# Attention and a residual MLP on one core: final evictions on VectorE in place, the pair's RELU in three parts, a PSUM tile for each Y product, u of batch 0 kept on the chip

## The chip, the core and the metric

The kernel runs on one NeuronCore of a Trainium2 chip. The core has a matrix engine (TensorE, PE in the profile, with its weight loads as PEld), a vector engine (VectorE, DVE), a scalar engine (ScalarE, ACT), GpSimd (POOL) and SyncE (SP), which here only starts transfers. Each engine works through its own list of instructions in order and waits at semaphores for the others. Transfers are started from SP's list (most of them) and from POOL's (those that also turn f32 into bf16). The metric is the device time of one execution, in microseconds (us).

## The reference

For each of 8 batches, 16 query heads and 4 key and value heads of 64 columns attend over 384 tokens; the result x is 384 x 1024. An MLP with two residuals follows.

```python
a1 = alpha1 * x + beta1
tok = np.einsum('ts,bsd->btd', w_tok, a1)
u = x + lam * tok
a2 = alpha2 * u + beta2
ch = np.maximum(a2 @ w_ch1, 0.0) @ w_ch2
return (u + lam * ch).astype(np.float32)
```

w_ch1 is 1024 x 4096, w_ch2 is 4096 x 1024. All inputs and the output are f32 in HBM.

## The kernel before

The two products with w_ch1 and w_ch2 are most of the work. The attention of a batch up to u (function `side`) is cut into small pieces that are put between the matmuls of an earlier batch's MLP. The places are written out by hand in a table `plan`: its key is a stage, a phase (0 for w_ch1, 1 for w_ch2) and a slot, and each `yield` of `main` or `pair` is one slot. The order of every engine's list is the order in which the Python code runs.

The program in time: a lead (attention of batch 0), `main(0)` and `main(1)` (MLP of batches 0 and 1), then `pair(0)`, `pair(1)`, `pair(2)` (MLP of batches 2 and 3, 4 and 5, 6 and 7). A `pair` takes two batches through a product as a 2 x 2 block matrix, by seven block products instead of eight; the numbers 1 to 7 in `SEQ1` and `PLACE2` are these products. The sums of blocks that they need are made by DVE: `sums_a` for the activations, `sum_w1` for w_ch1, `sum_w2` for w_ch2. The sums of w_ch2 are written to HBM once (`w2s`), and each pair fetches them (`fetch`).

Phase 0 of a pair has 8 groups g of 14 slots. A slot is one product o for one of two columns e of blocks: four matmuls into PSUM. Products 1, 6, 5 and 3 go on adding into one tile X[e]; after 1, 6 and 5 ACT copies what is there so far (`snap`, line L612), and the next product may only then write on. Products 7 and 4 add into Y, and product 2 uses Z. DVE adds snaps to Y and Z and writes the results into `hid` (L614, L616, L620). At the end of a group one ACT instruction applies RELU to three blocks of both columns (L627), and DVE forms two more blocks (L628, L629). The ring of six slots `w1` holds chunks of w_ch1 (POOL loads, L170) or blocks of w2s (SP fetches, L577); `free` takes the next load from `queue` as soon as a slot's last matmul is written down.

Phase 1 has the seven products in order 1, 5, 6, 3, 7, 4, 2, each as two halves h of three row tiles ms: 84 slots of four matmuls. Products 3, 7, 4 and 2 end an output block. For each ms DVE takes the product out of PSUM (L668, or L670 with a snap added). What is left of the final step runs on POOL: times lam (L671, not for product 3) and plus u (L672). Then SP stores the tile (L474). The three u tiles are loaded by SP at the start of the half h = 1 (L470). For the last output block of the last pair, DVE does L671 and L672 too.

In phase 1 `side` of two batches runs between the products. For each of its eight parts p: scores (PE, L265), exp (ACT, L274), `av` (PE, L304, then four DVE instructions, L309 to L319), `tok_flip` (PE, L329, then DVE L336 and L340). SP then stores u (`spill`, L229) and starts a transpose by DMA into `ops` (L353). The tile behind L340 has two buffers, so L340 of part p waits until the transpose of part p - 2 has landed. `sums_a` (L531 to L534) reads the transposed blocks. `load_next` loads q, k and v of a batch on POOL's list, and `put_flips` places their transposes on SP's list (L157, L161).

## Time and profile before

| What | Before |
|---|---|
| Median of 3 runs (lowest, highest) | 913.31 us (910.75, 914.59) |
| The profiled execution | 914.28 us, its span 912.5 us |
| Mean granted TensorE clock of that execution | 0.954 |
| Busy: ACT, POOL | 348.5 us, 231.7 us |
| Moved by DMA | 165.66 MB, mean 182 GB/s |

The span runs from the first to the last instruction. Busy time of PE comes from matmuls that overlap, so a full PE stands for matmuls back to back and not for the engine's peak. A wait is shown as the idle time of an engine ahead of an instruction, with the instruction that ended it behind an arrow. A granted clock under 1.00 means that TensorE was given fewer clock pulses in that stretch.

### The profile page before, as it was taken

To read this page: it belongs to the slowest core of one execution; us is meant where nothing else is said; L and a number is where in the kernel's file an instruction comes from. 1 tells how busy PE (TensorE), PEld (TensorE's weight loads), DVE (VectorE), ACT (ScalarE), POOL (GpSimd) and SP (SyncE) were. 2 spreads that over 40 slices of the span, in tenths; PEclk is the share of its full clock that TensorE was granted. 3 is DMA by queue.
4 is the path that set the end of the run, shared out by engine and by line. 5 is a ranking of instruction groups with operands and counts; after the bars stand their busy time and mean duration, and the time that the engine had idled before them with its cause. 6 is when DMAs were issued, how large, how long until landed. Compare 5 with 4: busy or idle time off the path is not lost. (4 is left out here: it accounts for less than half of the span.)

```text
span 912.5 us, 14496 instructions
## 1 busy us (share of the span) xinstructions
PE 765.9 (84%) x5707; PEld 418.8 (46%) x5707; DVE 495.9 (54%) x918; ACT 348.5 (38%) x465; POOL 231.7 (25%) x247
## 2 busy tenths in 40 slices
PE   8899998988958777999667678899894777779994
PEld 5655554654534444454333344445452344444441
DVE  7553562554786655486435655537664665554113
ACT  7422324643304555543210355564331145552100
POOL 8333204202003110003553531000434431100352
PEclk9999999999988999999977799999998889999998
DMA  9999999999978972468989998426887977725675
GB/s 191 207 210 203 221 197 217 208 213 214 291 212 165 212 93 92 143 199 220 234 226 168 166 145 114 113 94 191 205 270 222 179 117 93 93 93 172 214 252 191
DMA packets 231136, 165.66 MB, mean 182 GB/s; under 512 B 93588, under 2 KB 203780, under 8 KB 231068
## 3 DMA queue, kind: packets, MB, share of 16 engines
q0 software_dynamic: 114688, 54.37, 46.6%
q1 hardware_dynamic: 115836, 109.98, 42.2%
q8 instruction: 44, 0.72, 0.3%
q10 hardware_dynamic: 544, 0.39, 0.1%
q14 instruction: 24, 0.20, 0.1%
HBM read 166.63 MB, written 39.85 MB: 226 GB/s over the span
## 5 line engine op out<-in xcount | busy, mean ns | idle before, releaser
L647 PE MATMUL C<-w,arena 128*128 128x512 bf16 x1008 | 239.9, 385 | 1.5 <-DMA w<-w2s 1.5
L274 ACT ACTIVATE es<-sc 128x1024 bf16<-128x1024 f32 x126 | 121.8, 1022 | 201.7 <-PE sc L265 192.6
L647 PEld LDWEIGHTS <-arena 128*128 128x128 bf16 x1008 | 93.1, 99 | 107.6 <-issue 13.1
L612 ACT ACTIVATE hT<-X,bias 128x384 f32<-128x384 f32 x144 | 80.9, 577 | 102.4 <-PE X L607 83.6
L170 POOL DMA_DIRECT2D w<-in_moe_w_ch_dram x68 | 60.4, 892 | 218.2 <-PE X L607 161.2
L607 PEld LDWEIGHTS <-w 128*128 128x128 bf16 x768 | 76.3, 100 | 73.5 <-issue 21.6
L607 PEld LDWEIGHTS <-ws 128*128 128x128 bf16 x576 | 57.3, 99 | 105.4 <-issue 72.6
L607 PE MATMUL X<-ops,ws 128*128 128x384 bf16 x384 | 73.9, 337 | 27.8 <-ACT hT L612 27.8
L487 PE MATMUL h<-ops,w 128*128 128x384 bf16 (+1 forms) x480 | 87.5, 336 | 10.9 <-DMA ops<-a 3.9
L517 PE MATMUL ch<-arena,hT 128*128 128x512 bf16 x384 | 91.5, 383 | 1.5 <-DMA arena<-in_moe_w_ch_dram 1.5
L607 PE MATMUL X<-ops,w 128*128 128x384 bf16 x384 | 73.1, 334 | 14.7 <-DVE o L523 9.1
L627 ACT ACTIVATE arena<-arena 128x2304 bf16<-128x2304 bf16 x24 | 50.9, 2123 | 76.4 <-DVE arena L620 76.4
L660 POOL TENSOR_TENSOR hT<-hT 128x512 f32<-128x512 f32 x9 | 13.4, 1493 | 215.4 <-ACT hT L658 215.4
L487 PEld LDWEIGHTS <-w 128*128 128x128 bf16 x480 | 46.2, 100 | 43.8 <-issue 9.6
L672 POOL TENSOR_TENSOR o<-o,ut 128x512 f32<-128x512 f32 x33 | 45.0, 1371 | 79.6 <-DMA ut<-us 63.8
L607 PE MATMUL Y<-ops,ws 128*128 128x384 bf16 x192 | 39.0, 325 | 24.3 <-DVE arena L620 24.3
L304 PEld LDWEIGHTS <-es 128*128 128x128 bf16 x1008 | 39.6, 99 | 42.1 <-issue 31.0
L517 PEld LDWEIGHTS <-hT 128*128 128x128 bf16 x384 | 35.2, 98 | 39.9 <-issue 5.2
L614 DVE TENSOR_TENSOR arena<-Y,hT 128x384 bf16<-128x384 f32 x48 | 26.8, 558 | 44.0 <-ACT hT L612 41.8
L265 PE MATMUL sc<-qT,kT 64*128 64x384 bf16 (+2 forms) x576 | 45.5, 276 | 5.7 <-DVE xr L312 2.9
L340 DVE TENSOR_TENSOR a<-xr,vecs 128x384 bf16<-128x384 f32 x56 | 38.3, 685 | 20.1 <-DMA ops<-a 18.2
L607 PE MATMUL Y<-ops,w 128*128 128x384 bf16 x192 | 42.1, 342 | 8.5 <-DVE ops L534 5.3
(128 smaller groups left out, 908.9 us busy)
## 6 DMA issues: line engine op xcount, KB each, us to landing
w<-w2s SPq DMA_DIRECT2D x84, 512.0 KB, 4.1
w<-in_moe_w_ch_dram POOLq DMA_DIRECT2D x68, 512.0 KB, 8.9
ut<-us SPq DMA_DIRECT2D x48, 256.0 KB, 6.2
out_dram<-o SPq DMA_DIRECT2D x48, 256.0 KB, 2.1
us<-xr SPq DMA_DIRECT2D x56, 192.0 KB, 4.0
arena<-in_moe_w_ch_dram POOLq DMA_DIRECT2D x16, 512.0 KB, 19.9
w2s<-arena SPq DMA_DIRECT2D x24, 256.0 KB, 6.9
w2s<-ws SPq DMA_DIRECT2D x24, 256.0 KB, 4.1
```

Source lines behind the costliest of these rows:

```text
L170: nc.gpsimd.dma_start(out=w1[:, w1_slots[c]], in_=w1src[:, :, c * CW * P:(c + 1) * CW * P])
L265: nc.tensor.matmul(out=sc[:, hh, k % 4:k % 4 + n], lhsT=kT[r, 2 * p // G, BLK[hh][sk], :], rhs=qT[r, p, st:st + n, :], start=True, stop=True)
L274: nc.scalar.activation(out=e, in_=sc, func=EXP, scale=scale_qk)
L304: nc.tensor.matmul(out=av[:, hh, sq, :], lhsT=ess[k // 4][:, m % 2, k % 4, :], rhs=vb[:, sk, hk, :], start=(sk == 0), stop=(sk == NST - 1))
L340: nc.vector.tensor_tensor(out=a2s[p], in0=u, in1=bc(al2, p), op=MUL)
L487: nc.tensor.matmul(out=ps[:, :n], lhsT=w1[:, w1_slots[c], dt, j * P:(j + 1) * P], rhs=a2T[:, dt, :n], start=(dt == 0), stop=(dt == NDT - 1))
L517: nc.tensor.matmul(out=ps, lhsT=hT[:, nt, ms * P:(ms + 1) * P], rhs=w2[:, row(nt)[0], row(nt)[1], cs], start=(i == 0), stop=(i == NNT - 1))
L607: nc.tensor.matmul(out=ps, lhsT=tb[g, o][:, dt, e * P:(e + 1) * P], rhs=opb(LEFT1[o])[:, dt], start=(o in (1, 2, 7) and dt == 0), stop=(dt ...
L612: nc.scalar.activation(out=snap[o, e], in_=ps, func=IDENT, bias=hi if o == 5 else lo)
L627: nc.scalar.activation(out=hid[:, ts, 0:3], in_=hid[:, ts, 0:3], func=RELU)
L647: nc.tensor.matmul(out=X[ms], lhsT=hid[:, t, LEFT2[o], ms * P:(ms + 1) * P], rhs=ring[:, slot, t % 4 * 512:(t % 4 + 1) * 512], start=(o in ...
L672: fin(out=t, in0=t, in1=ut[ms], op=ADD)
```

## The change

1. Final step of phase 1: L671 and L672 go from POOL to DVE for all pairs, and the last add writes into the u tile itself, which is then stored. `main` does its last add in the same way. Tile `o` has two buffers instead of three.
2. The tiles `ut` and `ws` (five buffers) become six pieces of one tile `pad`, taken in turn. Ahead of that, `pad` is the home of batch 0's u: it is not stored to HBM any more, nor loaded again by `main(0)`. In `main(1)` a u tile is loaded in its own unit of 32 matmuls, and no longer one unit ahead.
3. Phase 0 of a pair: Y[0] and Y[1] are two tiles instead of two halves of one. The RELU becomes three: ACT on block 1 after product 3, DVE on block 2 after product 4 (a new TENSOR_SCALAR), ACT on block 0 in the next group's second slot (`finish`), together with the DVE subtraction that needs it.
4. `sum_w2`: all eight rows r move later. r = 0 and 1 go from phase 0 to phase 1 of `main(1)`, where r = 2 to 5 stood; r = 4 to 7 now run in the first four groups of `pair(0)`, one r in each (before, r = 6 and 7 took two groups each).
5. `load_next` and the transposes of a pair's first batch go to phase 0 of the pair before (slots 4 and 80 to 88), and the loads of its second batch to slot 100. For batch 4 both come out of phase 1 of `main(1)`.
6. `side` in the pairs takes 3.8 slots for a part instead of 4.2, and the second batch begins at slot 38 instead of 40, so the last `sums_a` stands in slot 77 instead of 82.
7. The first two chunks of w_ch1 for the next pair are queued two places earlier, ahead of the last two fetches.

```diff
+    pad = const.tile([P, 2 * NST * DM], bf, tag="pad", name="pad")
+    def piece():
+        i = turn[0] % 6
+        turn[0] += 1
+        return pad[:, i * 1024:(i + 1) * 1024]
...
-                spill(p)
                 return
...
                 for j in range(9):
-                    put(int(4.2 * j), scores2, j)
+                    put(int(3.8 * j), scores2, j)
                 for p in range(NP):
-                    put(int(4.2 * (p + 1)) + 3, av, p)
-                    put(int(4.2 * (p + 1)) + 6, tok_flip, p)
+                    put(int(3.8 * (p + 1)) + 3, av, p)
+                    put(int(3.8 * (p + 1)) + 6, tok_flip, p)
...
     def load_u(b, ms, dw):
-        t = sb.tile([P, 512], f32, tag="ut", name="ut", bufs=5)
+        t = piece().bitcast(f32)
...
-                if i == 8 and k + 1 < len(units):
-                    ut[units[k + 1]] = load_u(b, units[k + 1][1], units[k + 1][0])
+                if i == 0:
+                    get_u(k)
...
-    queue = [m for i in range(NB) for m in [(load_w1, c) for c in order1[0 if i else RING:]] + [(fetch, i, n) for n in range(SLOTS)]]
+    queue = [m for i in range(NB) for m in [(load_w1, c) for c in order1[2 if i else RING:]]
+             + [(fetch, i, n) for n in range(SLOTS - 2)] + [(load_w1, c) for c in order1[:2] if i + 1 < NB]
+             + [(fetch, i, n) for n in range(SLOTS - 2, SLOTS)]]
...
+        def finish(ts):
+            nc.scalar.activation(out=hid[:, ts, 0], in_=hid[:, ts, 0], func=RELU)
+            tt(out=hid[:, ts, 2], in0=hid[:, ts, 0], in1=hid[:, ts, 2], op=SUB)
+
         for g in range(NH // 2):
-            X, snap = {}, {}
-            Y = pairs["sc"].tile([P, 2, 512], f32, tag="sc", name="Y", bufs=2)
+            X, Y, snap = {}, {}, {}
...
+                if o == 7:
+                    Y[e] = pairs["sc"].tile([P, 2, 512], f32, tag="sc", name="Y", bufs=2)[:, 0]
...
-                if k == len(SEQ1) - 1:
-                    ts = slice(2 * g, 2 * g + 2)
-                    nc.scalar.activation(out=hid[:, ts, 0:3], in_=hid[:, ts, 0:3], func=RELU)
+                ts = slice(2 * g, 2 * g + 2)
+                if k == 1 and g:
+                    finish(slice(2 * g - 2, 2 * g))
+                if (o, e) == (3, 1):
+                    nc.scalar.activation(out=hid[:, ts, 1], in_=hid[:, ts, 1], func=RELU)
+                if (o, e) == (4, 1):
+                    nc.vector.tensor_scalar(out=hid[:, ts, 2], in0=hid[:, ts, 2], scalar1=0.0, scalar2=None,
+                                            op0=mybir.AluOpType.max)
                     tt(out=hid[:, ts, 3], in0=hid[:, ts, 2], in1=hid[:, ts, 1], op=ADD)
-                    tt(out=hid[:, ts, 2], in0=hid[:, ts, 0], in1=hid[:, ts, 2], op=SUB)
                 yield 0
+        finish(slice(NH - 2, NH))
...
-                            fin = tt if last and o == 2 else PL
...
-                                fin(out=t, in0=t, in1=lam_c, op=MUL)
-                            fin(out=t, in0=t, in1=ut[ms], op=ADD)
-                            store(b0 + bb, ms, dw * 512, (dw + 1) * 512, t)
+                                tt(out=t, in0=t, in1=lam_c, op=MUL)
+                            tt(out=ut[ms], in0=t, in1=ut[ms], op=ADD)
+                            store(b0 + bb, ms, dw * 512, (dw + 1) * 512, ut[ms])
...
-                where = (1, 0, 4 + 32 * r + 7 * i) if r < 2 else (1, 1, 12 * (r - 2) + 3 * i) if r < 6 else (2, 0, 28 * (r - 6) + 1 + 6 * i)
+                where = (1, 1, 12 * r + 3 * i) if r < 4 else (2, 0, 14 * (r - 4) + 1 + 3 * i)
...
-            put(ps, 0, 20, load_next, c + 1)
+            put(ps, 0, 4, load_next, c)
+            put_flips(ps, 0, c, range(80, 90, 2))
+            put(ps, 0, 100, load_next, c + 1)
             put_all(ps, 1, side(c)[1])
-            put_flips(ps, 1, c + 1, range(34, 39))
-            put_all(ps, 1, side(c + 1)[1], lambda u: u + 40)
+            put_flips(ps, 1, c + 1, range(31, 36))
+            put_all(ps, 1, side(c + 1)[1], lambda u: u + 38)
             for j in range(4):
-                put(ps, 1, 40 + int(4.2 * (j + 5)) + 9, sums_a, j)
+                put(ps, 1, 38 + int(3.8 * (j + 5)) + 9, sums_a, j)
```

Three places show how the lists change. A row is an instruction with its line, its output and its inputs; "x2" stands for two of the same in a row. The lines of the changed kernel are numbered anew: L612 becomes L632, L618 L638, L620 L640, L670 to L672 become L694 to L696.

ACT at the turn of a group of phase 0 in the last pair, before (snaps into hT, RELU of product 3's block, RELU of three blocks):

```order
L612 ACTIVATE hT<-X,bias_74 128x384 x6
L618 ACTIVATE arena<-X,bias_74 128x384 x2
L627 ACTIVATE arena<-arena 128x2x1152
L612 ACTIVATE hT<-X,bias_74 128x384 x6
L618 ACTIVATE arena<-X,bias_74 128x384 x2
```

And now:

```order
L638 ACTIVATE arena<-X,bias_74 128x384 x2
L649 ACTIVATE arena<-arena 128x2x384
L632 ACTIVATE hT<-X,bias_74 128x384 x2
L611 ACTIVATE arena<-arena 128x2x384
L632 ACTIVATE hT<-X,bias_74 128x384 x4
```

The long RELU between the last product of a group and the next group's first snap is gone; one short RELU stands ahead of the first two snaps and one behind them.

DVE at the end of phase 1 of the first pair, from the last part of `side` to the first sum of w_ch1, before:

```order
L534 TENSOR_TENSOR ops<-ops 128x384
L670 TENSOR_TENSOR o<-C,hT 128x512
L336 TENSOR_TENSOR xr<-one,xr 128x384
L340 TENSOR_TENSOR a_5673<-xr,vecs 128x384
L670 TENSOR_TENSOR o<-C,hT 128x512
L570 TENSOR_TENSOR ws<-w_71 128x1024
L565 TENSOR_TENSOR w_71<-w_71 128x1024
L570 TENSOR_TENSOR ws<-w_71,ws 128x1024 x2
L531 TENSOR_TENSOR ops<-ops 128x384
```

And now:

```order
L344 TENSOR_TENSOR xr<-one,xr 128x384
L348 TENSOR_TENSOR a_5571<-xr,vecs 128x384
L543 TENSOR_TENSOR ops<-ops 128x384
L544 TENSOR_TENSOR ops<-ops 128x384
L545 TENSOR_TENSOR ops<-ops 128x384
L546 TENSOR_TENSOR ops<-ops 128x384
L694 TENSOR_TENSOR o<-C,hT 128x512
L695 TENSOR_TENSOR o<-o,vecs 128x512
L696 TENSOR_TENSOR pad<-o,pad 128x512
```

The last part of `side` and the last sums of activations now come ahead of the last output block, and each tile of that block takes three DVE instructions in a row instead of one.

POOL in phase 1 of the first pair, before (its list goes on like this to the end of the phase):

```order
L661 TENSOR_TENSOR hT<-hT 128x512
L672 TENSOR_TENSOR o<-o,ut 128x512 x2
L130 DMA k_5015<-in_k_dram 128x4x192 x2
L154 DMA q_raw<-in_q_dram 128x4x192 x4
L149 DMA v_68<-in_v_dram 128x4x64 x3
L672 TENSOR_TENSOR o<-o,ut 128x512
L671 TENSOR_TENSOR o<-o,vecs 128x512
```

And now, from the same place to the first loads of the next pair:

```order
L686 TENSOR_TENSOR hT<-hT 128x512
L178 DMA w_71<-in_moe_w_ch_dram 128x8x256 x6
L138 DMA k_5669<-in_k_dram 128x4x192 x2
L162 DMA q_raw<-in_q_dram 128x4x192 x4
L157 DMA v_68<-in_v_dram 128x4x64 x3
```

POOL computes nothing there any more; the loads of the next batch stand behind those of w_ch1.

More of the change, by code (lines that the diff above doesn't have):

```diff
@@ L514, in main @@
             ps = bank([P, 512], "mm", "ch")
-            o = sb.tile([P, 512], f32, tag="o", name="o", bufs=3)
+            o = sb.tile([P, 512], f32, tag="o", name="o", bufs=2)
             for i, nt in enumerate(nts):
@@ L523, in main @@
             nc.vector.tensor_tensor(out=o, in0=ps, in1=lam_t[:, cs], op=MUL)
-            nc.vector.tensor_tensor(out=o, in0=o, in1=ut.pop((dw, ms)), op=ADD)
-            store(b, ms, dw * 512, (dw + 1) * 512, o)
+            u = ut.pop((dw, ms))
+            nc.vector.tensor_tensor(out=u, in0=o, in1=u, op=ADD)
+            store(b, ms, dw * 512, (dw + 1) * 512, u)
             yield 1
@@ L555, in sum_w2 @@
         else:
-            t = sb.tile([P, 1024], bf, tag="ut", name="ws", bufs=5)
+            t = piece()
         kept[o] = v = t.rearrange("p (a c) -> p a c", a=2)
@@ L613, in pair @@
                 if o == 5:
-                    tt(out=hid[:, t, 1], in0=Y[:, e, :S], in1=snap[5, e], op=ADD)
+                    tt(out=hid[:, t, 1], in0=Y[e][:, :S], in1=snap[5, e], op=ADD)
                 elif o == 2:
@@ L664, in pair @@
                             lam_c = lam_t[:, dw * 512:(dw + 1) * 512]
-                            t = sb.tile([P, 512], f32, tag="o", name="o", bufs=3)
-                            fin = tt if last and o == 2 else PL
+                            t = sb.tile([P, 512], f32, tag="o", name="o", bufs=2)
                             if o == 3:
@@ L724 @@
             nc.scalar.dma_start(out=qst[:, h:h + 2], in_=q[0, h:h + 2].rearrange("h (p st) d -> p h st d", st=NST))
-        xs[0] = arena[:, 10 * 2048:13 * 2048].bitcast(f32).rearrange("p (st d) -> p st d", st=NST)
+        xs[0] = pad.bitcast(f32).rearrange("p (st d) -> p st d", st=NST)
         qgs = [qst] + [sb.tile([P, G, NST, D], bf, tag="es", name="qg", bufs=EB) for _ in range(Hkv - 1)]
```

17 lines of the change are left out of this document (8 added, 9 removed).

## The prediction

> **What bounds the kernel now.** I read the clock and the span first, then cut the span at the stage borders that the timeline shows: first matmul of each pair, first matmul of its phase 1, last matmul. The rows give the stretch, its length, the busy time of PE, PEld, DVE, ACT and POOL (each with its count), the granted clock, the DMA share and GB/s.
>
> ```profile
> span 912.5 us, 14496 instructions
> ...
> 140.00:273.50 133.50, 114.54 (x1021) 65.80 (x1021) 76.25 (x153) 52.03 (x68) 20.61 (x26) 0.96 1.17 226
> 273.50:369.90 96.40, 78.21 (x449) 44.56 (x449) 56.21 (x99) 50.48 (x71) 15.45 (x19) 0.97 0.76 140
> 369.90:500.70 130.80, 106.68 (x913) 54.79 (x912) 71.22 (x128) 41.82 (x46) 38.87 (x34) 0.92 0.81 201
> 500.70:602.70 102.00, 79.75 (x448) 44.84 (x448) 60.35 (x101) 50.48 (x71) 26.48 (x27) 0.93 0.85 128
> 602.70:724.40 121.70, 104.66 (x914) 53.95 (x912) 71.76 (x128) 41.82 (x46) 32.58 (x25) 0.94 0.75 205
> 724.40:825.70 101.30, 77.80 (x449) 44.31 (x449) 60.26 (x101) 50.46 (x71) 19.79 (x18) 0.97 0.62 105
> 825.70:900.10 74.40, 72.85 (x336) 32.60 (x334) 17.35 (x22) 7.39 (x10) 25.54 (x21) 1.00 0.64 222
> 900.10:912.50 12.40, 0.00 (x0) 0.00 (x0) 4.66 (x7) 0.00 (x0) 0.98 (x1) 0.64 0.42 148
> ```
>
> The order is: `main(1)`, then phase 0 and phase 1 of each pair in turn, then the tail. No other engine comes near PE, but PE is not full: it is idle for 18 to 24 us in each phase 0, and for 24 and 17 us in the first two phases 1. The last phase 1, which has no attention in it, is nearly full (72.85 of 74.40). The table of waits names what ended PE's idle time (total us, times, longest):
>
> ```profile
> PE one L304 <- DVE xr L336: 28.0, 6, 11.7
> PE X L607 <- ACT hT L612: 27.8, 21, 1.3
> PE Y L607 <- DVE arena L620: 24.3, 24, 1.1
> PE X L607 <- DVE o L523: 9.1, 1, 9.1
> ```
>
> The middle two are phase 0. The timeline of one group of the last pair shows them (start, length, and in brackets the idle time ahead of it):
>
> ```profile
> 742.64 0.81 PE L607 MATMUL Y<-ops,ws 128*128 128x384 bf16 x4 [1.07 <-DVE arena L620]
> ...
> 754.45 0.81 PE L607 MATMUL Y<-ops,ws 128*128 128x384 bf16 x4 [1.07 <-DVE arena L620]
> ...
> 755.30 0.56 DVE L620 TENSOR_TENSOR arena<-Y,hT 128x384 bf16<-128x384 f32 x1 [0.90 <-PE Y L607]
> 755.89 2.12 ACT L627 ACTIVATE arena<-arena 128x2304 bf16<-128x2304 bf16 x1 [3.19 <-DVE arena L620]
> ...
> 757.92 1.03 ACT L612 ACTIVATE hT<-X,bias 128x384 f32<-128x384 f32 x2
> ...
> 758.53 1.46 PE L607 MATMUL X<-ops,ws 128*128 128x384 bf16 x8 [1.32 <-ACT hT L612]
> ```
>
> From 742.64 to 754.45 a group takes 11.81 us. PE loses 1.07 of it because Y of column 1 waits until DVE has read Y of column 0, and 1.32 because the first snap (the two copies at 757.92) stands behind the 2.12 us RELU on ACT. Both come back in every group: 24.3 and 27.8 us.
>
> In phase 1 the row for L336 is the larger loss. The SP list and POOL explain it:
>
> ```profile
> SPq L474 <- POOL o L672: 112.4, 28, 8.9
> ...
> POOL o L672 <- DMA ut<-us: 63.8, 8, 14.7
> ```
>
> One case in full:
>
> ```profile
> 467.26 3.16 SPq L470 DMA_DIRECT2D ut<-us  x3
> ...
> 474.71 1.26 POOL L672 TENSOR_TENSOR o<-o,ut 128x512 f32<-128x512 f32 x1 [8.79 <-DMA ut<-us]
> ...
> 476.00 0.34 SPq L474 DMA_DIRECT2D out_dram<-o  x1
> ...
> 477.05 1.27 SPq L353 DMA_TRANSPOSE ops<-a  x1
> ...
> 479.44 0.36 DVE L531 TENSOR_TENSOR ops<-ops 128x384 bf16<-128x384 bf16 x1 [10.62 <-DMA ops<-a]
> ...
> 481.98 1.15 PE L304 MATMUL one<-v,es 128*128 128x65 bf16 x18 [11.58 <-DVE xr L336]
> ```
>
> The u loads go out at 467.26, POOL's last step waits for them, the store behind it holds SP's list until 476.00, so the transpose L353 behind the store starts at 477.05. DVE has stood in front of `sums_a` for 10.62 us, and PE has waited 11.58 us for the DVE instruction behind that. The root is POOL: it does in 1.37 us what DVE does in 0.69, and SP waits 112.4 us for it.
>
> **The change part by part.** Durations used below:
>
> ```profile
> L628 DVE TENSOR_TENSOR arena<-arena 128x768 bf16<-128x768 bf16 x24 | 13.4, 558 | 52.5 <-ACT arena L627 52.5
> L672 POOL TENSOR_TENSOR o<-o,ut 128x512 f32<-128x512 f32 x33 | 45.0, 1371 | 79.6 <-DMA ut<-us 63.8 <-issue 14.4
> L672 DVE TENSOR_TENSOR o<-o,ut 128x512 f32<-128x512 f32 x3 | 2.1, 692 | 4.6 <-DMA ut<-us 4.5
> L618 ACT ACTIVATE arena<-X,bias 128x384 bf16<-128x384 f32 x48 | 27.8, 580 | 17.9 <-PE X L607 16.2
> L558 DVE TENSOR_TENSOR ws<-arena 128x1024 bf16<-128x1024 bf16 x12 | 8.2, 684 | 0.0
> L532 DVE TENSOR_TENSOR ops<-ops 128x384 bf16<-128x384 bf16 x12 | 4.3, 358 | 0.4
> ...
> L627 ACT ACTIVATE arena<-arena 128x2304 bf16<-128x2304 bf16 x24 | 50.9, 2123 | 76.4 <-DVE arena L620 76.4
> ...
> w<-in_moe_w_ch_dram POOLq DMA_DIRECT2D x68, 512.0 KB, 8.9
> ut<-us SPq DMA_DIRECT2D x48, 256.0 KB, 6.2
> ```
>
> *Y tiles and RELU (phase 0).* In the new lists the first matmul of product 4, column 1, carries no wait, and Y of column 0 is needed again only two products later; the 1.07 goes. A RELU of 768 elements lies on the line through 384 (0.58) and 2304 (2.12): 0.58 + 384 x 0.80 ns = 0.89 us. ACT then has per group six snaps of 0.58, two L618 and two RELUs of 0.89: 6.4 us. The first snap follows its matmul at once. The second RELU sits between the snaps of products 1 and 6, where I count some 0.5 us of slack before product 5 needs the snap of 6. So the 1.32 goes too, and a group takes 11.81 - 1.07 - 1.32 = 9.42 us. DVE gains one TENSOR_SCALAR that no row shows; 0.36 (half the elements) and 0.56 (as many, two inputs) bound it, and I take 0.56, the row of its size. DVE now has 60.3 / 8 = 7.5 us per group, so 8.1 of 9.42: it stays below PE, and the price is covered. Eight groups are 75.4, with 1 us to begin: 76.5 for the phases 0 that took 102.0 and 101.3.
>
> *Sums of w_ch2 in the first pair.* Four L558 of 0.684 per group in four groups: DVE has 8.1 + 2.7 = 10.8, more than PE. In order, with a write of the sums to wait for now and then, I take 11.3 (between 10.8, and 11.8 as before), the other four 9.42, and 5 us for the beginning, where the clock is low as before: 45.2 + 37.7 + 5 = 88 instead of 96.4. The seven SP issues of each row r lie on a list that has nothing else to do there.
>
> *Final step on DVE (phase 1 of pairs 0 and 1).* DVE gets 3 + 9 x 2 = 21 instructions of 0.69, or 14.5 us, per pair: 71.2 + 14.5 = 85.7. POOL loses as many, SP's stores no longer wait for POOL, the transposes go out on time, and the waits of up to 11.7 us vanish. PE's busy time is 106.7 and 104.7, of which some 5 and 2.5 us are slow clock after the long waits:
>
> ```profile
> 482.00:486.00 4.00, 4.00 (x31) 1.94 (x31) 3.25 (x5) 0.53 (x1) 2.27 (x2) 0.50 1.41 188
> 486.00:490.00 4.00, 3.65 (x21) 1.74 (x20) 0.54 (x2) 1.41 (x2) 0.04 (x1) 0.86 0.71 175
> ```
>
> Here PE is busy for 4.00 us at half clock and 3.65 at 0.86; 4 x 0.5 + 3.65 x 0.14 = 2.5 us lost. The floor is thus about 102. What is late next: DVE now waits for u itself. The loads go out when h = 1 begins and land 6.2 us later; DVE wants the first tile after eight matmuls (1.7 us at 72.85 / 336 = 0.217), some 1.5 us of attention and two instructions of 0.69, so at 4.6: 1.6 us of waiting in each of four blocks, 6.5 in all, with the part of `side` behind it held too. Another 3.5 I take for `sums_a`, three slots behind its transpose. 102 + 10 = 112, for 130.8 and 121.7. Below: 102, if all is hidden; above: the old lengths.
>
> *Placement.* Earlier `side`, earlier loads of w_ch1 and later sums leave the seam between pairs to DVE: two final tiles and four sums. It is inside the 112. Moving q, k and v in front of the w_ch1 loads on POOL's list (nine issues) costs nothing while those wait for PE anyway.
>
> *The beginning.* The last row of the table of waits, 9.1 us, is PE waiting for DVE at the end of `main(1)`. Five transposes leave SP's list there, DVE's load stays. I take 4 us for 9.1, and 2 us of slow clock saved: 133.5 becomes 126.5. Batch 0's u (eight stores, six loads less) is hidden behind PE: 0.
>
> *Last phase 1 and tail.* Without attention the u tile is wanted at 1.7 + 1.4 = 3.1 and lands at 6.2; PE takes its next tile 5.2 us after the first, so it loses some 0.5 per block: 74.4 becomes 76. In the tail the u tiles land 1 us after the last matmul, then seven DVE instructions of 0.69, then what follows the last one:
>
> ```profile
> 908.56 0.69 DVE L672 TENSOR_TENSOR o<-o,ut 128x512 f32<-128x512 f32 x1
> ```
>
> From 909.25 to 912.5 are 3.3 us: 1 + 4.8 + 3.3 = 9, instead of 12.4.
>
> *Sum.* 140 (to the end of `main(0)`, unchanged) + 126.5 + 88 + 112 + 76.5 + 112 + 76.5 + 76 + 9 = 816.5. The profiled execution took 914.28, 1.8 more than its span, and the median of the runs (913.31) is 1.0 less than that: 817.
>
> The Trainium skill, "TensorE: Matmul & The Clock Gate", section "What's actually happening", says that the clock is halved after an idle window of about 3.4 us and comes back after about 3.4 us of work. By that a long wait costs 1.7 us of slow clock and not 2.5; four such waits would give back 3 us less, and the sum would be 820. The rows at 482 to 490 show the longer recovery, so I stay with them.
>
> **Rivals.**
>
> *DVE becomes the bound in phase 1.* Between slots 38 and 84 nearly all of the 85.7 us of finals, sums and the second batch's `side` fall together; I count 53 us of DVE against 55 of PE. If every wait of DVE then holds PE, the two phases stay near their old lengths (126 on average): 817 + 28 = 845. For it: in order, a wait for u is paid in full. Against it: the 10.62 us that DVE stood idle in this very stretch before.
>
> *Loads of w_ch1 bound phase 0.* A chunk lands 8.9 us after its issue; the ring gives it one group and a bit. At 9.42 instead of 11.81 this may be late in the five loading groups of three pairs: 15 x 2.39 = 36, so 853. Against it:
>
> ```profile
> POOL w L170 <- PE X L607: 161.2, 13, 62.4
> ```
>
> POOL waits that long for PE to free slots; the DMA share in these phases is 0.62 to 0.85, where `main(1)` runs at 1.17. The Trainium skill, "SBUF — State Buffer", section "SBUF: two separate sides", warns that a DVE instruction that uses both of its ports locks GpSimd out, and with it the descriptors of GpSimd's DMAs. The new TENSOR_SCALAR may be one; no run here shows it, and it could only add to this rival.
>
> *The RELU wait stays.* If the first snap is still late (ACT waits for DVE inside the new RELU, and the snap of product 6 behind it), 27.8 us stay: 845.
>
> *Slower.* DVE takes over POOL's waits for u as they are: 63.8 us in 8, 8.0 each. If PE stood still that long at each of the 12 final blocks, 12 x 8 = 96 us would eat the 96 us that the sum gains: from 8 us per block the change loses, and with the slow clock behind each (2.5) it ends near 940. Against it: those 8 us were mostly u loads stuck behind SP's stores, which now wait for an engine twice as fast.
>
> **How the numbers follow.** Forecast 0.70, DVE bound 0.14, w_ch1 loads 0.07, RELU wait 0.04, slower 0.05. The likeliest gives 817. The low end is 817 less the 20 us of waits that I put into phases 1 and the 4 of the first pair's sums: 793. The high end takes in the first and third rival: 850. A change under 0.5% can't be told from none here; only a mixture of the last case would land there: faster 0.94, same 0.01, slower 0.05.
>
> **What would show it.** Group turns of 9.4 us in phase 0 of the last two pairs, without idle time of PE ahead of Y and X; if not, which of the two releasers is left tells which part failed. No wait of SP for POOL, and POOL's busy time in phase 1 down by some 78 us over the run (57 instructions of 1.37). No PE wait over 4 us in phases 1, the granted clock above 0.97 for the whole run. A DVE wait for the u load of 1 to 3 us per final block; more than 5 would be the slower rival. PE waiting for a DMA into w in phase 0 would be the second rival. The forecast is wrong if the phases 1 stay above 120 us or the groups above 11 us.

## The result and the profile after

The changed kernel takes 836.49 us (median of four runs, 833.16 to 838.74) where the kernel before takes 913.82 (910.75 to 914.59): a ratio of 0.9157, 95% interval 0.9119 to 0.9194. The profiled execution took 836.88 us with a span of 835.1. The forecast was 817 with a range of 793 to 850: the time lies in the range, 19.5 us above the number. The stages show that this is the sum of a large miss in one direction and a smaller one in the other.

The stages of the changed kernel, cut at the same borders as before: `main(0)`, `main(1)`, then phase 0 and phase 1 of each pair, and the tail (stretch, its length, busy time of PE, PEld, DVE, ACT and POOL, granted clock, DMA share, GB/s).

```profile
0.00:131.10 131.10, 127.45 (x1171) 76.79 (x1181) 78.02 (x182) 53.84 (x82) 51.28 (x77) 1.00 1.33 198
131.10:252.90 121.80, 112.08 (x1017) 66.02 (x1025) 72.04 (x145) 51.81 (x68) 20.63 (x26) 0.97 1.11 206
252.90:339.80 86.90, 80.02 (x449) 45.93 (x449) 62.15 (x114) 48.75 (x80) 15.43 (x19) 0.92 1.03 198
339.80:468.90 129.10, 106.92 (x901) 55.17 (x917) 83.69 (x154) 40.52 (x47) 15.67 (x14) 0.95 0.77 204
468.90:545.10 76.20, 74.00 (x445) 43.78 (x445) 57.86 (x105) 47.82 (x79) 20.65 (x27) 0.98 1.17 171
545.10:671.60 126.50, 107.05 (x897) 54.89 (x913) 82.95 (x153) 39.93 (x46) 12.95 (x12) 0.95 0.77 202
671.60:748.30 76.70, 73.11 (x449) 43.66 (x448) 58.51 (x106) 48.35 (x80) 10.03 (x12) 1.00 0.82 137
748.30:829.10 80.80, 74.47 (x331) 33.16 (x335) 28.83 (x42) 5.60 (x10) 7.50 (x6) 0.98 0.64 224
829.10:835.10 6.00, 0.00 (x1) 0.00 (x0) 2.73 (x5) 0.00 (x0) 0.00 (x0) 0.90 0.28 107
```

The phases 0 (86.90, 76.20, 76.70) are what was forecast. The two phases 1 with attention (129.10, 126.50) are together as long as before (130.80, 121.70). The one group of the last pair that the prediction spoke of now looks like this (timeline; start, length, in brackets the idle time ahead):

```profile
689.80 0.81 PE L627 MATMUL Z<-ops,w 128*128 128x384 bf16 x4
...
692.43 0.83 ACT L649 ACTIVATE arena<-arena 128x768 bf16<-128x768 bf16 x1
...
694.73 0.36 DVE L651 TENSOR_SCALAR arena<-arena 128x768 bf16<-128x768 bf16 x1
...
698.90 0.81 PE L627 MATMUL Z<-ops,w 128*128 128x384 bf16 x4
```

From Z to the next Z are 9.10 us, and no matmul in between carries a bracket: PE is full. The table of waits (total us, times, longest) shows where PE still stands idle, and what DVE and SP wait for:

```profile
PE one L312 <- DVE xr L344: 22.0, 12, 4.7
PE one L337 <- DVE a L327: 14.9, 7, 3.1
...
DVE pad L696 <- DMA pad<-us: 26.6, 10, 5.2
...
SPq L481 <- DVE pad L696: 82.2, 27, 6.1
```

SP's wait for POOL (112.4 us before) is gone, and POOL's busy time fell from 231.7 to 154.2. In its place SP waits 82.2 us for DVE's last step, DVE stands in front of the u tile for 26.6 us, and PE waits 36.9 us (22.0 and 14.9) for two attention instructions on DVE. The first of these waits was 28.0 us before (PE for DVE's L336), in fewer and longer pieces. One case in full, from the second pair's phase 1:

```profile
621.53 1.38 SPq L477 DMA_DIRECT2D pad<-us  x3
...
623.36 0.69 DVE L695 TENSOR_TENSOR o<-o,vecs 128x512 f32<-128x512 f32 x1
...
627.10 0.69 DVE L696 TENSOR_TENSOR pad<-o,pad 128x512 f32<-128x512 f32 x1 [3.05 <-DMA pad<-us]
627.71 0.55 DVE L344 TENSOR_TENSOR xr<-one,xr 128x384 f32<-128x384 f32 x1
...
628.32 0.71 PE L312 MATMUL one<-v,es 128*128 128x65 bf16 x18 [4.42 <-DVE xr L344]
```

The load of u goes out at 621.53; DVE reaches the last step at 624.05, waits 3.05 us for it, and L344 of the attention, which needs nothing of u, stands behind. PE loses 4.42.

### The profile page after: what moved, and what is told of

Read it like the earlier page. It is cut to its first block, busy times and chain, and to the rows that moved or that the text cites. A ratio compares the mean times of both kernels' runs of the same rounds, so it can differ in the third digit from the quotient of the medians.

```text
span 835.1 us, 14468 instructions
## 1 busy us (share of the span) xinstructions
PE 755.1 (90%) x5648; PEld 419.4 (50%) x5707; DVE 526.8 (63%) x999; ACT 336.6 (40%) x489; POOL 154.2 (18%) x190
## 4 chain that ended last, share of the span: by engine, by line
PE 65%; DMA 15%; DVE 12%; issue 3%; SPq 2%; ACT 1%; POOL 0%; DVEq 0%; ACTq 0%; POOLq 0%
PE C L672 18%; PE X L627 13%; PE h L494 7%; DMA pad<-us 7%; PE Y L627 7%; PE ch L528 5%; PE sc L273 4%; PE Z L627 3%; DMA ops<-a 2%; DMA arena<-in_moe_w_ch_dram 2%; DMA w2s<-hT 2%; PE one L312 2%; DVE xr L344 2%; PE one L337 1%; PE sc L337 1%
## 5 line engine op out<-in xcount | busy, mean ns | idle before, releaser
L672 PE MATMUL C<-w,arena 128*128 128x512 bf16 x967 | 238.2, 391 | 9.0 <-DVE o L694 4.7
L672 PEld LDWEIGHTS <-arena 128*128 128x128 bf16 x1008 | 94.7, 100 | 116.6 <-issue 24.6
L632 ACT ACTIVATE hT<-X,bias 128x384 f32<-128x384 f32 x144 | 83.4, 581 | 135.3 <-PE X L627 120.6
L627 PEld LDWEIGHTS <-w 128*128 128x128 bf16 x768 | 76.2, 99 | 72.4 <-issue 19.6
L528 PE MATMUL ch<-arena,hT 128*128 128x512 bf16 x366 | 88.0, 382 | 1.4 <-DMA arena<-in_moe_w_ch_dram 0.5
L494 PE MATMUL h<-ops,w 128*128 128x384 bf16 (+1 forms) x480 | 83.5, 327 | 1.3 <-ACT hT L502 1.1
L627 PEld LDWEIGHTS <-pad 128*128 128x128 bf16 x576 | 57.6, 100 | 41.8 <-issue 6.0
L627 PE MATMUL X<-ops,pad 128*128 128x384 bf16 x384 | 72.0, 330 | 1.4 <-ACT hT L632 1.4
L337 PEld LDWEIGHTS <-wtokT 128*128 128x128 bf16 x576 | 37.9, 99 | 32.3 <-DVE a L327 21.7
L627 PE MATMUL Z<-ops,w 128*128 128x384 bf16 x192 | 40.3, 334 | 6.7 <-DVE arena L636 6.7
L627 PE MATMUL Y<-ops,w 128*128 128x384 bf16 x192 | 40.0, 332 | 4.6 <-DVE w L577 4.4
L312 PE MATMUL one<-v,es 128*128 128x65 bf16 x576 | 23.6, 196 | 22.0 <-DVE xr L344 22.0
L696 DVE TENSOR_TENSOR pad<-o,pad 128x512 f32<-128x512 f32 x36 | 24.9, 692 | 27.5 <-DMA pad<-us 26.6
```

Of the source, the lines that this page charges most:

```text
L312: nc.tensor.matmul(out=av[:, hh, sq, :], lhsT=ess[k // 4][:, m % 2, k % 4, :], rhs=vb[:, sk, hk, :], start=(sk == 0), stop=(sk == NST - 1))
L337: nc.tensor.matmul(out=ps[:, tt, :], lhsT=wtokT[:, st, tt * P:(tt + 1) * P], rhs=a1s[p][:, st, :], start=(st == 0), stop=(st == NST - 1 an ...
L494: nc.tensor.matmul(out=ps[:, :n], lhsT=w1[:, w1_slots[c], dt, j * P:(j + 1) * P], rhs=a2T[:, dt, :n], start=(dt == 0), stop=(dt == NDT - 1))
L528: nc.tensor.matmul(out=ps, lhsT=hT[:, nt, ms * P:(ms + 1) * P], rhs=w2[:, row(nt)[0], row(nt)[1], cs], start=(i == 0), stop=(i == NNT - 1))
L627: nc.tensor.matmul(out=ps, lhsT=tb[g, o][:, dt, e * P:(e + 1) * P], rhs=opb(LEFT1[o])[:, dt], start=(o in (1, 2, 7) and dt == 0), stop=(dt ...
L632: nc.scalar.activation(out=snap[o, e], in_=ps, func=IDENT, bias=hi if o == 5 else lo)
```

## The experiments

All ran beside the kernel before (915.37, 913.36 and 913.63 us in three groups). A difference to the changed kernel below is taken between medians; each ratio to before has an interval of about 0.8% from end to end, so differences under 5 us are weak.

### u loaded earlier

```diff
-                if h and o in where:
+                if not h and o in where:
                     for ms in range(NST):
                         ut[ms] = load_u(...)
```

> The changed kernel, with the three u loads of each final product issued when its first half (h = 0) begins, one half product (some 9 us) earlier. Theory 'late u': what keeps the phases 1 long is the vector engine standing in front of the last step for u (26.6 us in all, 6.5 in each of the first two phases 1 and 13.3 in the last), with the attention's instructions behind it; then that wait falls below 4 us, the phases 1 go from 129 and 126.5 to about 121 and 119 and the last from 80.8 to 76: 836.9 - 8 - 8 - 5 = 816. Rival 'crowded vector engine': these waits are only where its slack shows (83 us of work in a dense stretch); the waits for u go, but PE waits as long for the attention's instructions, and the time stays at 830 to 837.

It took 810.78 us, ratio 0.888 [0.884, 0.8921]: 26 us less than the changed kernel, more than "late u" expected. The three phases 1 by themselves, the first waits of PE, DVE's wait for u, and ten microseconds near the end of the second phase 1:

```profile
338.90:457.55 118.65, 102.37 (x898) 53.86 (x913) 81.07 (x151) 39.95 (x46) 14.79 (x13) 0.99 0.87 223
535.80:653.10 117.30, 104.16 (x897) 54.24 (x912) 82.39 (x152) 39.95 (x46) 12.92 (x12) 0.97 0.87 223
730.40:803.50 73.10, 72.28 (x330) 32.76 (x335) 29.39 (x43) 5.58 (x10) 7.51 (x6) 1.00 0.71 248
...
PE one L312 <- DVE xr L344: 14.2, 12, 2.3
PE one L337 <- DVE a L327: 10.7, 5, 2.8
...
DVE pad L696 <- DMA pad<-us: 0.9, 1, 0.9
...
630.00:640.00 10.00, 5.74 (x53) 2.94 (x53) 9.59 (x21) 1.94 (x2) 0.00 (x0) 1.00 1.15 189
```

DVE's wait for u falls from 26.6 to 0.9 us. DVE does nearly the same work (81 and 82 us, for 84 and 83), yet the phases are 10.4, 9.2 and 7.7 us shorter. So the lateness of u made them longer, not DVE's amount of work. What remains is 25 us of waiting for attention instructions. At 630 to 640 DVE is busy for 9.59 of 10 us while PE has only 5.74 to do: there DVE's load is probably the bound, but no run takes work from DVE with all else unchanged.

### The final step back on GpSimd

```diff
+                            fin = tt if last and o == 2 else PL
 ...
-                                tt(out=t, in0=t, in1=lam_c, op=MUL)
-                            tt(out=ut[ms], in0=t, in1=ut[ms], op=ADD)
+                                fin(out=t, in0=t, in1=lam_c, op=MUL)
+                            fin(out=ut[ms], in0=t, in1=ut[ms], op=ADD)
```

> The changed kernel with the multiplication by lam (products 7, 4, 2) and the addition of u back on GpSimd, where the kernel before had them, all else as changed. Theory 'the final step gains nothing by itself': GpSimd's slowness is traded for a fuller vector engine, so the phases 1 stay within 4 us each of 129 and 126.5, and the time is 832 to 844. Rival 'it gains what the prediction said and the denser side work gives it back': without it the phases 1 go to 140 or more each, the wait of SP's list for GpSimd comes back (over 50 us), and the time is over 858.

It took 829.54 us, ratio 0.9078 [0.9039, 0.9117]. Neither expectation holds: with this part of the change undone the kernel is some 7 us faster. The two phases 1, and the waits that came back:

```profile
339.00:461.70 122.70, 104.19 (x898) 54.50 (x913) 78.94 (x136) 39.98 (x46) 32.72 (x25) 0.96 0.82 212
541.60:659.50 117.90, 105.64 (x897) 54.46 (x912) 79.03 (x137) 39.84 (x46) 34.22 (x27) 0.96 0.84 216
...
SPq L481 <- POOL pad L697: 100.4, 30, 8.2
DVE ops L543 <- DMA ops<-a: 19.3, 6, 6.8
```

SP waits 100 us for POOL again and DVE 19.3 for the transposes behind the stores, as in the kernel before (112.4 and 41.5); the phases are still 6.4 and 8.6 us shorter than the changed kernel's. POOL's wait for u (31.9 us here) delays stores; DVE's wait for u delays the attention.

### Both

> The changed kernel with both edits tried so far: u loads at h = 0, and the multiplication by lam and the addition of u on GpSimd. With early loads alone the time was 810.8, with GpSimd alone 829.5. Theory 'crowded vector engine': what PE still waits for (25 us in front of the attention's matmuls) is the vector engine at work on final steps; with 13 us of them on GpSimd it falls by about half, 798 to 806. Rival 'late u was all': with u early the vector engine no longer holds anything up, and on GpSimd the step only delays the stores and what SP's list holds behind them: 811 to 820.

The two edits above together took 826.89 us, ratio 0.905 [0.9025, 0.9075]. "Late u was all" is right in direction, and the step was dearer than it said:

```profile
SPq L481 <- POOL pad L697: 106.7, 31, 11.5
DVE ops L543 <- DMA ops<-a: 26.9, 6, 8.0
```

With these four kernels the step can be read as a table of two by two: with late loads POOL 829.5 and DVE 836.5, with early loads POOL 826.9 and DVE 810.8. The final step on DVE is worth 16 us when u is there, and costs 7 when it is not; early loads are worth 26 us to DVE and hardly anything to POOL. Why the phases 1 with POOL did not get shorter with early loads (126.4 and 124.4 us, for 122.7 and 117.9) stays open; it is not u, since POOL's wait for u fell from 31.9 to 1.0 us.

### The final step alone, on the kernel before

```diff
-                            fin = tt if last and o == 2 else PL
+                            fin = tt
```

> The kernel before with one part of the change: all final steps on the vector engine (u loads at h = 1, as both kernels have them). By the prediction's term this alone takes the two phases 1 from 130.8 and 121.7 to 112 each and the tail from 12.4 to 9: about 913 - 32 = 881. Theory 'late u', from the runs so far: the vector engine now stands in front of u with the attention behind it, which eats what SP's list gains: 905 to 918.

It took 923.04 us, ratio 1.0107 [1.007, 1.0145]: this part alone makes the kernel before slower, by 9.4 us. Its two phases 1 and DVE's wait for u:

```profile
368.20:500.20 132.00, 110.52 (x914) 55.74 (x912) 80.31 (x146) 41.81 (x46) 19.75 (x20) 0.94 0.82 202
603.60:734.40 130.80, 108.82 (x915) 55.31 (x913) 81.41 (x147) 41.82 (x46) 13.11 (x11) 0.95 0.75 196
...
DVE o L672 <- DMA ut<-us: 33.3, 10, 5.8
```

130.8 and 121.7 became 132.0 and 130.8, where the prediction's term said 112. "Late u" expected no gain; the loss lies 5 us beyond its end.

### The final step with early u, on the kernel before

> The kernel before with all final steps on the vector engine and the u loads at h = 0. Theory 'late u': the two edits need each other, and the prediction's term comes in only with both: phases 1 of 112 to 118 each and 72 to 73 in the last, 913 - 20 to 30 = 883 to 893. Rival 'seam': at the old spacing the last sums of the inputs (slot 82 of 84) hold the next phase 0, and less than 12 us is gained: over 901.

It took 897.65 us, ratio 0.9829 [0.979, 0.9868], in the gap between the two expectations; the rows show a part of each:

```profile
368.10:489.90 121.80, 107.10 (x914) 54.65 (x912) 79.39 (x143) 41.82 (x46) 19.67 (x20) 0.96 0.92 220
594.60:714.50 119.90, 107.36 (x914) 54.53 (x912) 79.71 (x144) 41.82 (x46) 13.06 (x11) 0.96 0.82 212
...
PE Y L607 <- DVE ops L534: 11.6, 2, 6.1
```

Against the same step with late u the phases 1 are 10.2 and 10.9 us shorter. The last row is the seam: in two phases 0 PE stands 11.6 us (5.3 in the kernel before) in front of the last sums of the inputs, which at the old spacing come at slot 82 of 84.

### The old spacing of the attention

```diff
-                for j in range(9):  put(int(3.8 * j), scores2, j)      # av, tok_flip: 3.8 too
+                for j in range(9):  put(int(4.2 * j), scores2, j)      # av, tok_flip: 4.2 too
-            put_flips(ps, 1, c + 1, range(31, 36))
-            put_all(ps, 1, side(c + 1)[1], lambda u: u + 38)
+            put_flips(ps, 1, c + 1, range(34, 39))
+            put_all(ps, 1, side(c + 1)[1], lambda u: u + 40)
-                put(ps, 1, 38 + int(3.8 * (j + 5)) + 9, sums_a, j)
+                put(ps, 1, 40 + int(4.2 * (j + 5)) + 9, sums_a, j)
```

> The changed kernel with the attention's slots in the pairs' phases 1 at the old spacing (4.2 instead of 3.8 slots, the second batch at slot 40 instead of 38, the flips at 34 to 38, the sums of the inputs last at slot 82 of 84). Theory 'density': the denser slots fill the vector engine's list; at the old spacing the phases 1 (129 and 126.5) get 3 to 6 us shorter each, 825 to 832. Rival 'seam': the later sums and transposes then run into the end of the phase, and the next phase 0 begins 3 to 6 us late, 838 to 848.

It took 852.08 us, ratio 0.9336 [0.9305, 0.9366], 15.6 more than the changed kernel and beyond the end of "seam". The phases 1 are unchanged (128.4 and 126.3); the loss is in the two phases 0 behind them, 8.6 and 8.5 us each, partly as low clock:

```profile
470.40:555.20 84.80, 76.64 (x449) 44.57 (x449) 62.09 (x114) 48.41 (x80) 21.48 (x28) 0.92 1.09 161
681.50:766.70 85.20, 76.83 (x449) 44.69 (x449) 62.16 (x114) 48.47 (x80) 8.81 (x11) 0.92 0.72 120
...
PE Y L627 <- DVE ops L544: 8.8, 2, 4.5
```

### Y in one tile again; RELU in one piece again

```diff
-            X, Y, snap = {}, {}, {}
+            X, snap = {}, {}
+            Y = pairs["sc"].tile([P, 2, 512], f32, tag="sc", name="Y", bufs=2)
 ...
-                if o == 7:
-                    Y[e] = pairs["sc"].tile([P, 2, 512], f32, ...)[:, 0]
```

> The changed kernel with one two-bank tile for the Y products of both columns again (RELU still in three parts). By the prediction's terms the wait of 1.07 us per group comes back alone: 24 groups, less the four of the first pair that the vector engine sets anyway: 836.9 + 20 to 26 = 857 to 863, with PE waiting for the vector engine ahead of Y some 20 to 25 us. Rival: Y's wait was only a consequence of the late first snap; then nothing comes back, 835 to 840.

```diff
-                if k == 1 and g: finish(...)
-                if (o, e) == (3, 1): nc.scalar.activation(... hid[:, ts, 1] ...)
-                if (o, e) == (4, 1): nc.vector.tensor_scalar(... hid[:, ts, 2] ...)
+                if k == len(SEQ1) - 1:
+                    nc.scalar.activation(out=hid[:, ts, 0:3], in_=hid[:, ts, 0:3], func=RELU)
+                    tt(out=hid[:, ts, 3], ...); tt(out=hid[:, ts, 2], ...)
```

> The changed kernel with one RELU of 2304 elements on the scalar engine per group again (a bank per Y product kept). By the prediction's terms the wait of 1.32 us per group ahead of X comes back alone: 21 to 24 times, 836.9 + 24 to 30 = 861 to 867. Rival: with Y in banks of its own PE runs so far ahead that the late snap is covered; less than 10 us comes back, 838 to 846.

They took 863.92 us (ratio 0.9438 [0.9387, 0.9489]) and 870.84 us (0.9535 [0.9493, 0.9578]): 27.4 and 34.4 more than the changed kernel. The row that each brings to the table of waits, Y first:

```profile
PE Y L626 <- DVE arena L639: 27.7, 24, 2.8
```

```profile
PE X L627 <- ACT hT L632: 35.6, 23, 2.3
```

Each wait comes back alone, in 24 and in 23 of the 24 groups. Both terms are shown. Y's time lies 0.9 us above its expectation and the RELU's 4 above; the latter's wait is now 1.5 us a group (35.6 / 23) and not 1.3.

### The beginning

```diff
                                      func=..., scale=al2T[:, p:p + 1])
+                spill(p)
 ...
-                where = (1, 1, 12 * r + 3 * i) if r < 4 else (2, 0, 14 * (r - 4) + 1 + 3 * i)
+                where = (1, 0, 4 + 32 * r + 7 * i) if r < 2 else (1, 1, 12 * (r - 2) + 3 * i) if r < 6 else (2, 0, 28 * (r - 6) + 1 + 6 * i)
```

> The changed kernel with two parts of its beginning undone: batch 0's u is stored to memory again (eight stores more on SP's list, by nobody read), and the sums of w_ch2 stand at their old places (two of eight rows in the first phase of main(1), two instead of four in the first pair). By the traces of the two kernels: the stall at 45 us (PE 3.4 us, behind the vector engine, behind the late rows of lam) and the one at 145 us (PE 3.5, behind SP's transposes) come back with some 2 us of low clock each; main(0) and main(1) take 8 to 16 us more, the first phase 0 of a pair 2 to 6 less: 840 to 848. Rival: the beginning's gain is from the earlier flips and the later loads; then 830 to 837.

It took 842.82 us, ratio 0.924 [0.9192, 0.9288], in the expected range. Here POOL clears the tile `rows` and SP issues the loads of lam's rows into it, first with the stores put back (PE's wait and SP's below), then in the changed kernel:

```profile
38.17 1.47 POOL L835 MEMSET rows<- 128x512 f32 x3
38.74 1.26 SPq L797 DMA_DIRECT2D rows<-in_moe_lam_dram  x2
...
45.80 1.47 PE L495 MATMUL h<-ops,w 128*128 128x385 bf16 x4 [4.87 <-DVE hT L505]
...
SPq L797 <- POOL rows L835: 5.0, 2, 4.8
```

```profile
33.54 1.47 POOL L834 MEMSET rows<- 128x512 f32 x3
34.11 1.19 SPq L796 DMA_DIRECT2D rows<-in_moe_lam_dram  x2
```

With the eight stores of u put back the rows go out 4.6 us later, DVE waits for them, and PE stands 4.87 us behind DVE. SP's list is not the reason: its last store is issued by 34.36, and then SP waits 4.8 us for POOL. In both kernels the rows go out 0.57 us after the MEMSET begins, and the MEMSET comes 4.6 us later because POOL's loads ahead of it do. Those wait for earlier loads to land, 13.1 us in all instead of 8.6. The DMA engines are busy all through this stretch in both kernels (a share of 1.3 and more); of what they move between 20 and 38 us, 1.31 MB are now u's, and POOL's loads get 2.39 MB instead of 3.46. So the stores cost what their bytes took from the loads.

`main(0)` ends at 137.8 instead of 131.1; in the kernel before at 139.3. The wait at 145 us did not come back: PE waits only 0.5 us for transposed activations there. So the expectation named one cause rightly and one wrongly. What removed the wait at 145 us would by elimination be the transposes and loads moved out of `main(1)`; no run undid these alone, so this is not shown. `main(1)` took 128.9 us and not 121.8; the first phase 0 took 76.0 and not 86.9, which is more than the 2 to 6 expected.

### Early u with the old places of the sums

> The changed kernel with u loads at h = 0 (810.8 so far) and the sums of w_ch2 at their old places (two rows in main(1)'s first phase, two instead of four in the first pair); batch 0's u stays kept. From the run with both parts of the beginning undone: main(1) takes 7 us more (loads of w_ch1 late behind the stores of the sums), the first pair's phase 0 11 us less, main(0) nothing: 804 to 809. Rival: the 7 us of main(1) were from the stores of u, and then it is 798 to 803; or the 11 us depend on them, then 812 or more.

It took 814.23 us, ratio 0.8921 [0.8888, 0.8954], not told apart from 810.78. It lies where the rival put it (812 or more), though not for the rival's reason. Its `main(1)` and its first phase 0:

```profile
131.00:265.20 134.20, 114.85 (x1025) 65.90 (x1024) 76.66 (x153) 51.81 (x68) 20.61 (x26) 0.97 1.11 215
265.20:341.70 76.50, 75.69 (x449) 44.63 (x449) 58.06 (x106) 48.50 (x80) 15.43 (x19) 0.97 0.98 179
...
PE h L494 <- DMA w<-in_moe_w_ch_dram: 7.2, 6, 2.4
```

The sums cost about as much in the one place as in the other: phase 0 is 8.9 us shorter than in the kernel with early u alone (85.4), `main(1)` 11.7 longer (122.5), where PE now waits for w_ch1. The expectation had 7 for the latter and missed; `main(1)` scatters here, with 128.9, 134.2 and 130.0 us in the three runs of the changed kernel that have the sums at these places. `main(0)` ends at 131.0 again, so the 6.8 us there belong to the stores of u.

### The last two instructions of the final step, later in DVE's list

```diff
+                            def rest(...):   # MUL by lam, ADD of u, store: run half a unit later
+                            rests.append(rest)
 ...
                         if t % 8 == 3:
                             yield 1
+                            while len(rests) > 0: rests.pop(0)()
```

The first run has u loaded where the changed kernel loads it:

> The changed kernel (u loads where it has them) with the final step split in its place in the vector engine's list: the instruction that reads the bank stays, the multiplication by lam and the addition of u come half a unit later (four matmuls on, behind the attention's instructions of that slot). Theory 'in-order wait for u': the wait for u then stands behind the attention's instructions and not ahead of them, and the load has 1 to 2 us more; of the 26 us that early loads gain some 12 to 20 come from this alone: 816 to 825. Rival: the wait only moves to the next attention link, 832 to 840.

820.45 us, ratio 0.9 [0.896, 0.904]: 16 us of the 26, as expected, but the waits tell it otherwise. In the two phases 1 with attention (121.3 and 120.4 us) DVE's wait for u did not move behind the attention; it fell from 6.5 and 6.3 us to 0.8 and 0.2, since half a unit later u is there. So the later place helped by the time that it gives the load, and what the order alone is worth with u still late is not shown. In the last phase 1 DVE still waits 12.3 us. The second run has early u and the old places of the sums:

> The same, with the multiplication by lam and the addition of u half a unit later in the vector engine's list, behind the attention's instructions of that slot. Theory 'order in the list': of the 25 us that PE still waits for attention with early loads, a part is one final step of 2.07 us ahead of a link of 2 us; with only 0.69 of it ahead, 5 to 10 us go: 796 to 803. Rival 'amount': near the end of a phase 1 the vector engine is busy for 9.6 of 10 us, the order then changes nothing, and the later stores cost as much: within 3 us of the kernel without it.

816.21 us, ratio 0.8944 [0.8906, 0.8982]: no difference to the kernel without it beyond the scatter, as "amount" said. PE's wait for the two attention instructions only fell from 24.9 to 22.4 us, and its wait at the start of a phase 0 for DVE to read the last product rose from 6.0 to 12.1. With u in time, this change of order gains nothing.

The fastest median is that of the changed kernel with early loads of u, 810.78 us: 0.888 of the kernel before, and 26 us below the changed kernel.

## Why the prediction was right, and where not

Stage by stage, in us, forecast and measured, and the kernel with early u beside them:

| stage | before | forecast | after | early u |
|---|---|---|---|---|
| to the end of `main(1)` | 273.5 | 266.5 | 252.9 | 253.5 |
| pair 0, phase 0 | 96.4 | 88 | 86.9 | 85.4 |
| pair 0, phase 1 | 130.8 | 112 | 129.1 | 118.7 |
| pair 1, phase 0 | 102.0 | 76.5 | 76.2 | 78.3 |
| pair 1, phase 1 | 121.7 | 112 | 126.5 | 117.3 |
| pair 2, phase 0 | 101.3 | 76.5 | 76.7 | 77.3 |
| pair 2, phase 1 | 74.4 | 76 | 80.8 | 73.1 |
| tail | 12.4 | 9 | 6.0 | 5.5 |
| span | 912.5 | 816.5 | 835.1 | 809.0 |

By the signs that it named itself, the forecast held in the phases 0 and failed in the phases 1. These were not to stay above 120 us, and took 129.1 and 126.5; PE was not to wait over 4 us there, and waited up to 4.7; the clock was to be above 0.97, and was 0.967. The three phases 1 together are 36.4 us over their numbers, which alone would give 853 and lie outside the range. The beginning (13.6 under), the tail (3.0 under) and the phases 0 (1.2 under) bring it back. That the time lies in the range is luck to this extent.

**Y tiles and RELU: right.** Both waits went, and each comes back with its own part undone. The group takes 9.10 us and not 9.42. The 0.32 are in the rows: a block of four matmuls is printed with 0.81 us, but with no wait the next one starts after 0.65 (689.80 to 690.45 above), so each of the two waits cost 0.16 more than its bracket. TENSOR_SCALAR took 0.36 (the lower bound; 0.56 was taken) and the RELU of 768 elements 0.83 (0.89 was interpolated). The phases came within 1.1 us of their numbers, but one term had no reason: before, a phase 0 had 102.0 - 8 x 11.81 = 7.5 us beside its groups, and the prediction put "1 us to begin" without naming what clears the rest. The old spacing shows it: 8.5 us per phase come back, so this is the gain of the earlier attention (item 6 of the change), which the prediction had left "inside the 112".

**Final step on DVE: the step that failed.** The prediction saw the wait and sized it well: 1.6 us in each of four blocks, 6.5 in all. Over its two phases DVE waited 6.5 and 6.3 us for u, each three times. What was wrong is what such a wait costs. It was added once to a floor of 102. But in each phase PE waited 19 and 18 us for attention instructions, and PE's busy time was 107, not 102, because the low clock behind long waits, which the floor took away, stayed. Taking the wait away (early u) gave 10.4 and 9.2 us back, and 0.04 and 0.02 of clock. The other part, 5 to 7 us per phase over 112, stays when u is in time: PE then still waits 13 and 12 us per phase for attention instructions, where the prediction allowed 3.5, for another reason. That three instructions of 0.69 stand in a row ahead of an attention instruction is not the cause: with two of them moved behind it the phases took 119.6 and 120.1 us, for 117.7 and 119.9. DVE's dense stretches are the likelier one, but that stays open.

The rival "DVE becomes the bound in phase 1" had a chance of 0.14, and in the phases 1 it is the case that came: it had the length (126 on average; 127.8 came) and, among its arguments, the mechanism ("in order, a wait for u is paid in full"). Its main reason was DVE's amount of work, and the runs show that with nearly the same work and u in time the phases are 118. Its sum, 845, was too high because the beginning gained more.

**SP's wait for POOL: true, and worth less.** It went as forecast, and with it the waits of up to 11.7 us. But the prediction called POOL's slowness the root of the long phases, and its own rows say otherwise: the L672 of its case had waited 8.79 us for u and then took 1.26. On POOL or on DVE, the step stood behind a late u. In the run with POOL on this step and denser slots, SP waits 100 us for POOL and the phases take 122.7 and 117.9.

**Last phase 1: mis-sized.** 76 was forecast, 80.8 came. In the timeline the loads went out as h = 1 began, and u came 6.3, 8.0 and 6.8 us after them, for 6.2 in the prediction; DVE stood there after 2.1 to 2.9 us, not 3.1. It waited 4.2, 5.2 and 4.0 us, and PE stood 1.1, 2.9 and 1.7 us in front of the bank of a second tile, which DVE had not yet read; 0.5 each had been forecast. With early u these waits are gone, and 7.7 us with them.

**Beginning: mis-sized the other way.** Batch 0's u was put at 0, "hidden behind PE". Nobody waited for its data, but its transfer took room from POOL's loads where the DMA engines had none to spare, and through them it delayed the rows of lam, on which DVE and then PE waited: 6.8 us in `main(0)`. `main(1)` took 121.8 where 126.5 was forecast; the sums of w_ch2 were priced where they went (the first pair's phase 0, 88 forecast, 86.9 measured), and not where they left: with them back in `main(1)`, PE waits 7.2 us for w_ch1 there. The tail took 6.0 for 9.

**Loads of w_ch1** held PE in no phase 0: the table of waits after has no such row.

Put together from the runs: undoing Y costs 27.4, RELU 34.4, the spacing 15.6, the beginning's two parts 6.3, and undoing the final step gains 7.0: 76.7, of the 77.3 that the change gains. That these close so well is partly luck: each carries some 4 us, the parts affect each other, as the two by two shows, and no run undid items 5 and 7 of the change alone.

## What to carry to other kernels

When a step is moved to a faster engine, move its loads as well: on an engine whose list others depend on, an instruction costs its length plus what its input is late, for everyone behind it. Price a removed DMA by what shares the DMA engines with it: a store that nobody waits for still takes bytes from the loads that somebody waits for. Before naming a slow engine as the root of a wait, look at what that engine itself was waiting for. And undo each part of a change that wins: here one of its parts lost 7 us, and one edit to the time of its loads turned that into a gain of 16.

## What the runs showed of the chip

The clock came back at different speeds. Two long waits of PE in the changed kernel's second phase 1 end at 628.3 and 657.3 us; the stretches behind them:

```profile
628.30:630.30 2.00, 1.93 (x21) 0.92 (x21) 1.72 (x4) 0.00 (x0) 0.00 (x0) 0.70 0.74 238
630.30:632.30 2.00, 2.00 (x12) 0.75 (x12) 1.93 (x4) 1.11 (x2) 0.00 (x0) 0.50 0.23 49
...
657.30:659.30 2.00, 2.00 (x21) 1.34 (x21) 1.93 (x4) 0.00 (x0) 0.00 (x0) 0.50 0.55 175
659.30:661.30 2.00, 2.00 (x6) 0.70 (x5) 1.90 (x5) 0.00 (x0) 0.00 (x0) 0.50 0.71 112
661.30:663.30 2.00, 1.82 (x6) 0.65 (x6) 1.69 (x5) 0.00 (x0) 0.00 (x0) 0.52 0.83 295
```

After the wait of 4.42 us some 1.6 us of work are lost (2 x 0.3 + 2 x 0.5), after the wait of 3.70 some 2.9 (2 x 0.5 + 2 x 0.5 + 1.82 x 0.48). The 2.5 us of the prediction lie between. The Trainium skill, "TensorE: Matmul & The Clock Gate", section "What's actually happening", lets the full clock come back after about 3.4 us of work; worked out from that figure, 1.7 us lost is an estimate. The first wait agrees, the second took longer. In the run with early u a wait of 2.30 us (PE idle at 637.75 to 640.05, with one of 1.85 us shortly before) was already followed by 4 us at 0.58 and 0.56. So two shorter waits close together can cost clock as well.
